# The last output tile in two column halves, and one store per block in the middle of a state-space and feed-forward kernel

## The chip, the cores and the metric

The kernel runs on one core of one Trainium2 chip. The metric is the device time of one execution in microseconds (us). The core has a matrix engine (TensorE, PE in the profile, with its weight loads listed apart as PEld), a vector engine (VectorE, DVE), a scalar engine (ScalarE, ACT), a general engine (GpSimd, POOL) and a queue processor (SyncE, SP) that here only issues DMAs. Each engine takes its instructions in the order in which the program lists them. The core's 16 DMA engines move data between the chip's main memory and the on-chip SBUF. PE writes its results to banks of PSUM, from where ACT or DVE copy them to SBUF.

## The reference

```
for each chunk of 32 tokens of each batch and head:
    L       = exp(cum_i - cum_j) for i >= j, else 0      # cum: running sum of log a
    y_intra = ((C B^T) * L) x
    y_inter = (C state) * exp(cum)
    y       = y_intra + y_inter
    state   = exp(sum of log a) * state + sum_j B_j x_j exp(cum_end - cum_j)

x   = y as (batch * tokens) x (heads * 32)               # 3072 x 256
out = (relu(x @ w_gate) * (x @ w_val)) @ w_out           # 256 -> 1536 -> 256
```

There are 4 batches, 8 heads, 768 tokens, head size 32 and state size 16. The result is 3072 x 256 in float32. The change touches only the last product, with `w_out`, and the way in which its result leaves the chip.

## The kernel before, in words

The 3072 tokens are cut into 6 blocks of 512 (`NBLK` = 6). For each block the feed-forward part computes the hidden activations `h` in 12 chunks of 128 (`gv` over 512 tokens, `gvh` over 256): PE makes gate and value in PSUM, ACT applies the relu (lines 600 and 615), and DVE multiplies (601 and 618). The first part, the state-space scan, runs over 12 pairs of 128-token chunks. Its pieces for the next block are set between the feed-forward pieces of the present one. POOL scales the loaded `B` and `C` (`scale_bc`, line 291), casts `x` (`cast_x`, line 307) and masks part of the products (`causal`, line 489).

The order of all instructions is written out by hand. The function `in_order` at the end ties each engine's instructions to the order in which the program lists them, so a reader can follow each engine from the text.

`fout(b, ts)` computes row group `ts` (128 tokens, four to a block) of block `b` of the output: 12 matmuls, one for each chunk of `h`. The chunk of `h` is the stationary operand, which is loaded anew for every matmul, and 256 columns of `w_out` stream through. Two row groups share a PSUM bank, except in the last block, where each has a bank of its own. Banks come from a rotation of five (`bank`).

`foevac(b, ts)` follows each `fout`. In blocks 1 to 4, ACT copies two row groups at once (line 652) to a buffer `ob`, and SP issues a store of 256 KB (line 653); this happens after row groups 1 and 3. In the last block each row group is copied alone (line 646), by ACT for groups 0 and 2 and by DVE for groups 1 and 3, and stored alone (line 647), 128 KB each, through ACT's DMA queue for groups 0 and 2 and through SP's for groups 1 and 3. The buffers `ob` rotate over three.

At the head of each block from 1 on, `load(n)` puts the loads of later pairs on SP's queue: six DMAs a pair (lines 116 and 117), for two pairs, up to pair 11. They are scaled by POOL some chunks later in the same block (`scale(P + 2)`) or in the next (`scale(Q)`). SP's queue is in order too, so the loads of block `b + 1` stand behind the stores of block `b`. Each DMA that SP or ACT issues adds to one of eight completion counters, which are used in rotation in the program's order. Before a DMA reuses a counter, its issuer waits for the DMA eight places earlier. At the end of the program (line 897 in the profile) SP waits for all eight counters, one after the other in their order, and then all engines meet at a barrier.

The main loop's skeleton, by which the steps can be followed:

```
for b in 1..5:
    loads of later pairs on SP
    gvh / gv chunks of block b, with transposes and scans of the next pairs between
    fout(b, 0), foevac(b, 0);  G, gevac of the next pair
    fout(b, 1), foevac(b, 1);  fout(b, 2), foevac(b, 2);  Dm, sums, yevac, G, states
    fout(b, 3), foevac(b, 3)
```

Of the kernel before, what the change touches and what calls it, by code (L numbers as in the profile page):

```python
# [8 lines left out]
FP32 = mybir.dt.float32  # L9
# [20 lines left out]
def kernel(  # L30
# [13 lines left out]
    nc = tc.nc  # L44
# [5 lines left out]
    DM, DF = moe_w_gate.shape  # L50
    T = NB * S
    NF = DF // 128
    NPAIR = T // 256
    PPB = NC // 2
    NBLK = T // 512
# [5 lines left out]
    ffn = ctx.enter_context(tc.tile_pool(name="ffn", bufs=2))  # L61
# [4 lines left out]
    def bank(name="bank", shape=(128, 512), dtype=FP32):  # L66
        return mm.tile(list(shape), dtype, tag="shared", bufs=NSHARED, name=name)
# [78 lines left out]
    for rows, base in ((slice(0, 128), 128), (slice(0, 64), 0)):  # L146
        nc.gpsimd.affine_select(
            out=wmask[rows], in_=wmask[rows], pattern=[[-1, 2], [1, 128]],
# [6 lines left out]
    for k in range(4):  # L155
# [16 lines left out]
        out=cp0, data0=a0, data1=zero1[0:R].to_broadcast([R, 128]), initial=1.0,  # L172
# [11 lines left out]
    wo = glob.tile([128, NF, DM], BF16)  # L184
# [402 lines left out]
    fst = {}  # L587
# [37 lines left out]
    def fout(b, ts):  # L625
        if ts % 2 == 0 or b == NBLK - 1:
            fst["o"] = bank("o", (128, 2, DM))
        o = fst["o"]
        for f in range(NF):
            nc.tensor.matmul(  # L630
                out=o[:, ts % 2], lhsT=fst[b][:, f, ts * 128:(ts + 1) * 128],
                rhs=wo[:, f], start=(f == 0), stop=(f == NF - 1),
                skip_group_check=True)

    def foevac(b, ts):
        last = b == NBLK - 1
        if ts % 2 == 0 and not last:
            if ts and not b:
                fst["ob"] = ob = ffn.tile([128, 2, DM], FP32, tag="ob", name="ob", bufs=3)
                nc.scalar.copy(out=ob[:, 0], in_=fst["o"][:, 0])  # L640
            return
        ob = fst.pop("ob", None) or ffn.tile([128, 2, DM], FP32, tag="ob", name="ob", bufs=3)
        r0 = b * 512 + ts * 128
        if last:
            i = ts % 2
            (nc.vector.tensor_copy if i else nc.scalar.copy)(out=ob[:, i], in_=fst["o"][:, i])
            (nc.sync if i else nc.scalar).dma_start(out=out[r0:r0 + 128, :], in_=ob[:, i])
            return
        if b == 0 and ts == 3:
            nc.scalar.copy(out=ob[:, 1], in_=fst["o"][:, 1])  # L650
        else:
            nc.scalar.copy(out=ob, in_=fst["o"])  # L652
        nc.sync.dma_start(
            out=out[r0 - 128:r0 + 128, :].rearrange("(i p) m -> p i m", p=128), in_=ob)
# [108 lines left out]
    copy_C(2, 1)  # L763
    cast_x(2, P_)
    fout(0, 0)
    foevac(0, 0)
    G_wide(2)
    adds(2)
# [9 lines left out]
    scale_bc(3, P_)  # L778
    cast_x(3, P_)
    fout(0, 1)  # L780
    foevac(0, 1)
    fout(0, 2)
    foevac(0, 2)
    inter_wide(2)
    D_wide(2)
# [116 lines left out]
```

## Time and profile before

| | |
|---|---|
| median of 6 runs | 128.15 us (127.32 to 128.64) |
| the profiled execution's own time | 127.72 us |
| its span, from first to last instruction | 126.0 us |
| PE busy | 119.6 us (95%) |
| DVE, ACT, POOL busy | 88.5, 81.7, 42.1 us |
| granted PE clock over the span | 1.000 |
| read from main memory, written to it | 11.13 MB, 3.15 MB |
| stores through SP after two row groups | 10, of 256 KB each, median 2.2 us from issue to landing |
| stores of the last block | 2 through ACT (2.1 us to landing), 2 through SP (1.7 us), 128 KB each |

A line of a group gives the source line, engine, operation and tiles, how many there were, the time in all in us and the mean of one in ns, and then the engine's idle time ahead of them with what ended it. `L630 PE` is the matmul in line 630, `L630 PEld` its weight loads. PE's records are pipelined: a matmul's record is longer than the distance to the next one, so distances are read from starts, or from the chain of waits, which is cut without overlap. A line of the timeline gives start and length in us, engine, line and operation, and in brackets the idle time before it and what released it.

### The profile page before, as it was taken

To read this page: it belongs to the slowest core of one execution; us is meant where nothing else is said; L and a number is where in the kernel's file an instruction comes from. 1 tells how busy PE (TensorE), PEld (TensorE's weight loads), DVE (VectorE), ACT (ScalarE), POOL (GpSimd) and SP (SyncE) were. 2 spreads that over 40 slices of the span, in tenths; PEclk is the share of its full clock that TensorE was granted. 3 is DMA by queue.
4 is the path that set the end of the run, shared out by engine and by line. 5 is a ranking of instruction groups with operands and counts; after the bars stand their busy time and mean duration, and the time that the engine had idled before them with its cause. 6 is when DMAs were issued, how large, how long until landed. Compare 5 with 4: busy or idle time off the path is not lost.

```text
span 126.0 us, 3627 instructions
## 1 busy us (share of the span) xinstructions
PE 119.6 (95%) x1382; PEld 83.7 (66%) x1388; DVE 88.5 (70%) x196; ACT 81.7 (65%) x184; POOL 42.1 (33%) x86
## 2 busy tenths in 40 slices
PE   6979899999999999999999999999999999999980
PEld 6856585478685478874577864577855678844870
DVE  3795888764799675989674888655988556787420
ACT  0467588835788934787935887745888647877310
POOL 6589864126535025801321704033500033000000
PEclk9999999999999999999999999999999999999999
DMA  3999999996988998597922499802200002200031
GB/s 65 208 173 203 161 219 196 156 112 79 106 96 218 111 116 90 167 122 85 105 40 88 101 107 110 104 8 83 88 0 0 0 0 88 83 0 0 5 121 46
DMA packets 72209, 12.15 MB, mean 96 GB/s; under 512 B 65936, under 2 KB 72192, under 8 KB 72192
## 3 DMA queue, kind: packets, MB, share of 16 engines
q1 hardware_dynamic: 66096, 8.91, 47.4%
q0 software_dynamic: 3184, 2.36, 12.6%
q10 hardware_dynamic: 2912, 0.66, 2.5%
q8 instruction: 11, 0.18, 0.6%
q14 instruction: 6, 0.05, 0.1%
HBM read 11.13 MB, written 3.15 MB: 113 GB/s over the span
## 4 chain that ended last, share of the span: by engine, by line
PE 85%; DMA 8%; ACT 2%; POOL 1%; issue 1%; DVE 0%; DVEq 0%; POOLq 0%
PE o L630 26%; PE gv L612 16%; PE val L597 14%; PE gate L594 12%; DMA wo<-in_moe_w_out_dram 8%; PE w L180 4%; PE y L569 2%; PE g L481 2%; PE tp L321 2%; PE y L558 1%; ACT gs L389 1%; PE g L372 1%; POOL gs L385 1%; PE A_ps L528 1%; PE y L462 1%
## 5 line engine op out<-in xcount | busy, mean ns | idle before, releaser
L601 DVE TENSOR_TENSOR h<-r,val 128x512 bf16<-128x512 bf16 x44 | 29.5, 686 | 8.8 <-ACT r L600 7.2
L630 PE MATMUL o<-wo,h 128*128 128x256 bf16 x288 | 34.2, 273 | 0.2 <-DMA wo<-in_moe_w_out_dram 0.2
L630 PEld LDWEIGHTS <-h 128*128 128x128 bf16 x288 | 27.1, 98 | 5.5 <-issue 1.5
L600 ACT ACTIVATE r<-gate 128x512 bf16<-128x512 f32 x44 | 25.9, 600 | 6.0 <-PE gate L594 4.0
L597 PE MATMUL val<-yT,wv 128*128 128x512 bf16 x88 | 26.2, 379 | 0.3
L594 PE MATMUL gate<-yT,wg 128*128 128x512 bf16 x82 | 24.9, 379 | 0.0
L618 DVE TENSOR_TENSOR h<-r,gv 128x256 bf16<-128x256 bf16 x56 | 22.5, 419 | 2.6 <-ACT r L615 1.6
L615 ACT ACTIVATE r<-gv 128x256 bf16<-128x256 f32 x56 | 21.4, 385 | 2.4 <-PE gv L612 0.4
L612 PE MATMUL gv<-yT,wv 128*128 128x256 bf16 x112 | 21.4, 273 | 0.6 <-DMA wv<-in_moe_w_val_dram 0.6
L612 PE MATMUL gv<-yT,wg 128*128 128x256 bf16 x112 | 21.4, 273 | 0.1
L489 POOL TENSOR_SCALAR_AFFINE_SELECT gs<-gs 128x512 bf16<-128x512 bf16 (+1 forms) x18 | 8.9, 520 | 32.8 <-ACT gs L500 32.8
L506 DVE TENSOR_TENSOR gs<-g,maskUT 128x512 bf16<-128x512 f32 x18 | 11.6, 686 | 11.7 <-issue 9.6
L291 POOL TENSOR_TENSOR bs<-bcr,scaleBC 128x256 bf16<-128x256 f32 x18 | 11.0, 630 | 20.5 <-PE val L597 6.0
L597 PEld LDWEIGHTS <-wv 128*128 128x128 bf16 x88 | 8.6, 98 | 10.4
L594 PEld LDWEIGHTS <-wg 128*128 128x128 bf16 x88 | 8.2, 98 | 7.0
L612 PEld LDWEIGHTS <-wv 128*128 128x128 bf16 x112 | 10.9, 98 | 2.1 <-DMA wv<-in_moe_w_val_dram 0.8
L612 PEld LDWEIGHTS <-wg 128*128 128x128 bf16 x112 | 10.2, 98 | 2.0 <-issue 0.2
L500 ACT CAST gs<-g 128x512 bf16<-128x512 f32 x9 | 5.3, 589 | 6.7 <-PE g L481 6.7
L582 ACT CAST yT<-y 128x512 bf16<-128x512 f32 x9 | 5.3, 586 | 5.3 <-PE y L569 2.7
L652 ACT COPY ob<-o 128x512 f32<-128x512 f32 x9 | 5.3, 584 | 4.1 <-PE o L630 4.1
L180 PE MATMUL w<-warm 128*128 128x128 bf16 x49 | 5.9, 296 | 1.0 <-DVE tmask L154 1.0
L180 PEld LDWEIGHTS <-warm 128*128 128x128 bf16 x58 | 5.3, 132 | 1.6 <-DVE tmask L154 1.0
(103 smaller groups left out, 118.3 us busy)
## 6 DMA issues: line engine op xcount, KB each, us to landing
out_dram<-ob SPq DMA_DIRECT2D x10, 256.0 KB, 2.2
xr<-in_x_dram SPq DMA_DIRECT2D x19, 128.0 KB, 3.7
bcr<-in_C_dram SPq DMA_DIRECT2D x19, 64.0 KB, 3.4
bcr<-in_B_dram SPq DMA_DIRECT2D x19, 64.0 KB, 3.8
wo<-in_moe_w_out_dram POOLq DMA_DIRECT2D x1, 768.0 KB, 10.7
xr<-in_x_dram SPq DMA_DIRECT2D x2, 256.0 KB, 8.0
wg<-in_moe_w_gate_dram POOLq DMA_DIRECT2D x1, 384.0 KB, 5.9
wv<-in_moe_w_val_dram POOLq DMA_DIRECT2D x1, 384.0 KB, 7.2
```

Of the source, the lines that this page charges most:

```text
L180: nc.tensor.matmul(out=w, lhsT=warm, rhs=rhs, start=True, stop=True)
L291: eng.tensor_tensor(out=bs.rearrange("s k (q t n) -> s k t q n", q=4, t=2)[:, :, t], in0=src[:, :, t], in1=f[:, :, 4 * t:4 * t + 4].to_bro ...
L489: nc.gpsimd.affine_select(out=dst, in_=dst, pattern=[[0, n], [1, 128]], compare_op=ALU.is_ge, fill=0.0, base=0, channel_multiplier=-1)
L506: nc.vector.tensor_tensor(out=d[:, q], in0=g[q], in1=m, op=ALU.mult)
L594: nc.tensor.matmul(out=g, lhsT=wg[:, k, fs], rhs=yT[:, k, tk], start=(k == 0), stop=(k == 1))
L597: nc.tensor.matmul(out=v, lhsT=wv[:, k, fs], rhs=yT[:, k, tk], start=(k == 0), stop=(k == 1))
L600: nc.scalar.activation(r, g, AF.Relu)
L601: nc.vector.tensor_tensor(out=fst[b][:, f], in0=r, in1=v, op=ALU.mult)
L612: nc.tensor.matmul(out=gv_[:, j], lhsT=w[:, k, fs], rhs=yT[:, k, tk], start=(k == 0), stop=(k == 1), skip_group_check=True)
L615: nc.scalar.activation(r, gv_[:, 0], AF.Relu)
L618: nc.vector.tensor_tensor(out=fst[b][:, f, u * 256:(u + 1) * 256], in0=r, in1=gv_[:, 1], op=ALU.mult)
L630: nc.tensor.matmul(out=o[:, ts % 2], lhsT=fst[b][:, f, ts * 128:(ts + 1) * 128], rhs=wo[:, f], start=(f == 0), stop=(f == NF - 1), skip_gr ...
```

## The change

In the last block, row group 3 (the last 128 tokens) is computed as two halves of 128 columns each: 12 matmuls for columns 0 to 127, then 12 for columns 128 to 255, with the chunk of `h` loaded for each. The second half has a PSUM bank of its own. ACT copies the first half and stores it through its own queue, and DVE copies the second half and stores it through SP's queue, 64 KB each, in rows of 512 bytes.

In blocks 1 to 3, ACT's two copies of a block go to one buffer `ob4` of four row groups (two such buffers in rotation), and SP issues one store of 512 KB after row group 3 in place of two of 256 KB after groups 1 and 3. Blocks 0 and 4 keep their two stores.

```diff
@@ fout(b, ts)
         if ts % 2 == 0 or b == NBLK - 1:
             fst["o"] = bank("o", (128, 2, DM))
         o = fst["o"]
+        if b == NBLK - 1 and ts == 3:
+            fst["oh"] = [o[:, 1, 0:128], bank("o", (128, 128))]
+            for i, oh in enumerate(fst["oh"]):
+                for f in range(NF):
+                    nc.tensor.matmul(
+                        out=oh, lhsT=fst[b][:, f, ts * 128:(ts + 1) * 128],
+                        rhs=wo[:, f, i * 128:(i + 1) * 128], start=(f == 0),
+                        stop=(f == NF - 1), skip_group_check=True)
+            return
         for f in range(NF):
@@ foevac(b, ts)
                 nc.scalar.copy(out=ob[:, 0], in_=fst["o"][:, 0])
             return
+        if 1 <= b <= 3:
+            if ts == 1:
+                fst["ob4"] = ffn.tile([128, 4, DM], FP32, tag="ob4", name="ob4")
+            ob = fst["ob4"]
+            nc.scalar.copy(out=ob[:, ts - 1:ts + 1], in_=fst["o"])
+            if ts == 3:
+                nc.sync.dma_start(
+                    out=out[b * 512:(b + 1) * 512, :].rearrange("(i p) m -> p i m", p=128),
+                    in_=ob)
+            return
         ob = fst.pop("ob", None) or ffn.tile([128, 2, DM], FP32, tag="ob", name="ob", bufs=3)
         r0 = b * 512 + ts * 128
+        if last and ts == 3:
+            for i, (eng, q) in enumerate(((nc.scalar.copy, nc.scalar),
+                                          (nc.vector.tensor_copy, nc.sync))):
+                cs = slice(i * 128, (i + 1) * 128)
+                eng(out=ob[:, 1, cs], in_=fst["oh"][i])
+                q.dma_start(out=out[r0:r0 + 128, cs], in_=ob[:, 1, cs])
+            return
         if last:
```

## The prediction

> **What bounds the kernel now.** I read the page's engine table first, then the chain of waits to its end, then the end itself in stretches.
>
> ```profile
> PE 119.6 (95%) x1382; PEld 83.7 (66%) x1388; DVE 88.5 (70%) x196; ACT 81.7 (65%) x184; POOL 42.1 (33%) x86
> ```
>
> TensorE (PE) is busy 119.6 us of 126.0, at full granted clock in every slice. From 100 us on, the chain of waits is one unbroken row of PE pieces; it ends like this (start, length, what):
>
> ```profile
> 116.33 0.43 PE gate L594 x2
> 116.76 0.43 PE val L597 x2
> 117.19 5.25 PE o L630 x48
> 122.45 0.03 DVEq L646
> 122.48 0.04 issue
> 122.53 0.42 DVE ob L646
> ```
>
> So two things can shorten this kernel: less PE time, or a shorter end behind the last matmul. The end is 126.0 - 122.5 = 3.5 us in which no engine computes except for one copy, as the busy time by stretch shows (after the stretch: length, then PE, PEld, DVE, ACT, POOL, clock, DMA share, GB/s):
>
> ```profile
> 122.00:123.00 1.00, 0.44 (x4) 0.14 (x2) 0.42 (x1) 0.00 (x0) 0.00 (x0) 1.00 0.39 131
> 123.00:124.00 1.00, 0.00 (x0) 0.00 (x0) 0.00 (x0) 0.00 (x0) 0.00 (x0) 1.00 0.15 51
> 124.00:125.00 1.00, 0.00 (x0) 0.00 (x0) 0.00 (x0) 0.00 (x0) 0.00 (x0) 1.00 0.24 80
> 125.00:126.00 1.00, 0.00 (x0) 0.00 (x0) 0.00 (x0) 0.00 (x0) 0.00 (x0) 1.00 0.00 0
> ```
>
> The trace's instruction and packet records split it: copy 122.53 to 122.95; SP starts the store at 122.98; its packets run from 123.83 to 124.34; SP's wait for it passes at 124.70; then SP checks the remaining completion counters of the DMAs one by one, about 0.06 us each, until 125.07; drains and the last barrier take until 125.96.
>
> **The change, part by part.**
>
> *The last tile's matmuls.* Twelve pairs of weight load and 256-column matmul become 24 pairs of weight load and 128-column matmul: the same columns, twice the loads. A 256-column pair costs 5.25/48 = 0.109 us. What a 128-column pair costs is the main question, because every such pair loads a full 128x128 tile of weights, and the loads' records last 98 ns. These rows hold the nearest case, transposes (128 columns, a new 128x128 weight tile each): first the groups, then one piece of the chain.
>
> ```profile
> L630 PE MATMUL o<-wo,h 128*128 128x256 bf16 x288 | 34.2, 273 | 0.2 <-DMA wo<-in_moe_w_out_dram 0.2
> L321 PE MATMUL tp<-ident,bs 128*128 128x128 bf16 x44 | 4.6, 223 | 0.0
> L321 PEld LDWEIGHTS <-bs 128*128 128x128 bf16 x48 | 3.5, 99 | 2.7
> ```
> ```profile
> 75.45 0.22 PE tp L321 x4
> ```
>
> Four pairs in 0.22 us: 55 ns each, although the load's record is 99 ns, so loads overlap each other's records and the matmuls. Seven warm-up pairs at 7.0 us start 55.6 to 56 ns apart in the records. With 55.6: 24 x 0.0556 = 1.334 against 12 x 0.109 = 1.31; +0.03 us. Here a rule speaks against the change. The Trainium skill, "TensorE: Matmul & The Clock Gate", section "Back-to-back issue gap", says that a sustained stream of load and matmul pairs runs at about 81 ns per 128-column matmul, and that the 56 ns gap leaves the loads out. By it the tile takes 24 x 0.081 = 1.94 us, +0.63. The row has loads in it and decides: I take 55.6 ns; 81 ns is an end of the range, since the row's bursts are 4 to 7 pairs and this one is 24.
>
> *The evacuations.* The first half is ready 12 pairs, 12 x 0.0556 = 0.67 us, before the second. ScalarE (ACT) is free after issuing the store of row group 2 (121.56 + 0.36 = 121.93); its half copy, between 164 ns for 6 columns (L224) and 373 ns for 256 (L646), is by straight line 0.27 us, done at 122.24, and its store starts near 122.27. It also waits for row group 0's store, whose buffer it reuses: issued at 118.94, last packet 120.98; passed by 121.4. Behind it on ACT stands only its own store. That half lies beside the second one, which sets the end. There VectorE (DVE) copies 128 columns in place of 256:
>
> ```profile
> L646 DVE COPY ob<-o 128x256 f32<-128x256 f32 x2 | 0.8, 425 | 4.0 <-PE o L630 4.0
> L667 DVE COPY wfac<-fac 128x48 f32<-128x48 f32 x1 | 0.2, 208 | 0.6 <-PE fac L209 0.6
> ```
>
> (425 - 208)/208 = 1.04 ns per column, so 425 - 128 x 1.04 = 0.291 us: -0.134. Bounds: -0.21 (half) to 0. In the program as built it waits on no ACT copy of this tile; if it did, ACT is done at 122.24, before the 122.55 at which DVE starts anyway.
>
> *The last store.* Still 128 rows, so I leave its issue (0.345 us) and the time to the first packet (0.85 us) as they are; each row has 512 B in place of 1024. In the packet records a 1024 B packet takes 46 ns and a 512 B one on the same queue (the 48 of the load of `a`) 25 to 27 ns. Eight packets on each of 16 DMA engines: 8 x 46 = 0.37 to 8 x 26 = 0.21 us, -0.16. Bounds: -0.2 to 0 (packets of half the size at the old duration).
>
> *The final checks.* Hardware DMAs count on eight counters in rotation, and SP's last checks go through these in order. Before, the last store counts on counter 1, checked at 124.70; six more checks follow it. The change removes three DMAs (blocks 1 to 3) and adds one: two fewer, so the last store moves from counter 1 to (1 - 2) mod 8 = 7, which is checked last. The other checks then lie under the wait. -(125.07 - 124.70) = -0.37 us. The first half's store is on counter 6, some 0.6 us ahead of the last. Bounds: -0.37 to 0, should the end be held by something else.
>
> *One store per block in blocks 1 to 3.* Each takes an SP issue and a 256 KB transfer away after row group 1 and makes the one after row group 3 512 KB. The copies on ACT stay, same sizes (0.58 us each). On SP nothing stood between the two stores, so nothing is passed; behind the larger one stand the next block's twelve loads (blocks 1 and 2). 256 KB more is 16 packets of 1 KB per engine, 16 x 46 = 0.74 us, so loads land up to 0.74 us later, by shared engines or by a counter's wait. Who notices? GpSimd (POOL), which scales them:
>
> ```profile
> 59.29 1.20 POOL L291 TENSOR_TENSOR bs<-bcr,scaleBC 128x256 bf16<-128x256 f32 x2 [5.96 <-PE val L597]
> 65.32 0.99 POOL L489 TENSOR_SCALAR_AFFINE_SELECT gs<-gs 128x512 bf16<-128x512 bf16 x2 [4.28 <-ACT gs L500]
> 77.22 1.20 POOL L291 TENSOR_TENSOR bs<-bcr,scaleBC 128x256 bf16<-128x256 f32 x2 [5.68 <-PE gate L594]
> 83.68 0.99 POOL L489 TENSOR_SCALAR_AFFINE_SELECT gs<-gs 128x512 bf16<-128x512 bf16 x2 [4.71 <-ACT gs L500]
> ```
>
> Both scalings wait for PE, not for data: the four loads they need have landed by 57.5 and 76.0, 1.8 and 1.2 us ahead. Past that, POOL idles 4.3 and 4.7 us before the mask that is queued next. Cost 0; without this cover, the 0.74 us twice. Gain also 0: no engine waits for these stores or for SP.
>
> *Sum,* on the profiled execution (127.72, span 125.96): +0.03 - 0.13 - 0.16 - 0.37 = -0.63 us, span about 125.3. What lies around the span stays. The median of the runs shown is 128.15, 0.43 above the profiled one; the difference carries over: 127.5 us.
>
> **Rivals.** A change of 0.5% (0.64 us) is about what a measurement of this kernel can tell from none.
>
> 1. *Part of the end doesn't come.* The final checks were not what held the end, or the half-sized packets bring nothing: 127.7 to 127.9. For it: both terms come from records of one execution. Against it: the six checks stand in a row with nothing else in flight.
> 2. *The weight loads show.* 81 ns per pair takes back 0.61 us: 128.1. For it: the rule above, no row with 24 such pairs. Against it: 55 ns in every burst.
> 3. *Slower: the weight loads bind.* If a pair cannot go below the 0.109 us that it takes now, the tile takes 2.62 us, +1.31, less 0.66 for the rest: 128.8. It decides from the pitch at which the tile's growth eats 0.66 us: (1.31 + 0.66)/24 = 82 ns. For it: 98 ns loads twice as often. Against it: the 55 ns row, whose loads are as long.
> 4. *The split or the merged stores do nothing:* a DVE half that waits for ACT, or loads that turn late. The first costs nothing by the times above; the second must exceed 1.2 + 4.7 us before a mask moves. About 128.15 if all else failed too.
>
> **How the numbers follow.** Likeliest (0.66): all terms near their values, 127.5, own range 127.1 to 127.8; its centre is on the 0.5% line (127.51), and I count 0.50 of it as faster, since no term is rounded up, and 0.16 as same. Rivals 1 and 4 0.15 and rival 2 0.09, nearly all same; rival 3 0.10, slower at 128.8. Faster 0.51, same 0.39, slower 0.10. The range for 8 in 10 runs from 126.9 (all bounds of the gains and a measurement's own spread) to 128.4 (past rival 2, short of rival 3).
>
> **What would show it.** Right: 24 matmuls of 128 columns 55 to 56 ns apart; DVE's last copy near 0.29 us from 122.55; the last store's landing at 1.5 us in place of 1.7; less than 1.0 us from SP's last DMA wait to the end in place of 1.26; POOL's scalings still released by PE. Wrong: a pitch of 80 ns or more, a last copy of 0.4 us, a wait of PE for POOL or a load in blocks 2 to 4, or an end after the landing as long as now.

## The result, and the profile after

The changed kernel takes 127.5 us (median of 35 runs, 126.87 to 128.47) against 128.28 us for the kernel before (72 runs). The ratio is 0.9944, with a 95% interval from 0.9931 to 0.9956: 0.72 us less, between 0.56 and 0.88. That is 0.56% less, by its middle value a little more than the 0.5% that the prediction took for the least that a measurement of this kernel can tell from none; the small end of the interval, 0.44%, lies below that. The time is the forecast one.

PE's share has not moved. From the page of the changed kernel:

```profile
PE 119.1 (95%) x1394; PEld 83.4 (66%) x1400; DVE 88.2 (70%) x196; ACT 82.2 (65%) x185; POOL 42.4 (34%) x86
```

The end of its chain of waits (start, length, what):

```profile
117.24 0.43 PE val L597 x2
117.67 3.93 PE o L639 x36
121.60 1.35 PE o L633 x24
122.96 0.04 DVEq L667
122.99 0.04 issue
123.03 0.29 DVE ob L667
```

The 24 pairs of 128 columns (line 633) take 1.35 us and the copy 0.29. Behind the last matmul only this copy is left, and the span ends at 125.8 in place of 126.0:

```profile
123.00:124.00 1.00, 0.00 (x0) 0.00 (x0) 0.29 (x1) 0.00 (x0) 0.00 (x0) 1.00 0.55 176
124.00:125.00 1.00, 0.00 (x0) 0.00 (x0) 0.00 (x0) 0.00 (x0) 0.00 (x0) 1.00 0.23 66
125.00:126.00 1.00, 0.00 (x0) 0.00 (x0) 0.00 (x0) 0.00 (x0) 0.00 (x0) 1.00 0.00 0
```

The two profiled executions didn't start alike. The first matmul of the output (row group 0 of block 0) starts at 25.34 us after and 24.86 before, in a part of the program that the change doesn't touch. In the ten executions whose traces are used here that start lies between 24.7 and 26.3. So spans are not compared here. What is compared is a distance inside the trace: from the first matmul of the last row group to the end. It is 4.999 us before and 4.370 after, 0.629 us less. Between block 0 and the last row group nothing changed: from the first output matmul of one block to that of the next it is 19.352, 18.561, 18.360, 18.324, 17.573 us before and 19.353, 18.561, 18.360, 18.321, 17.574 after.

The instruction and packet records split the 4.999 and the 4.370 us like this:

| step | before, us | after, us | difference | predicted |
|---|---|---|---|---|
| first matmul of the row group to the start of DVE's copy | 1.566 | 1.597 | +0.03 | +0.03 |
| DVE's last copy | 0.425 | 0.291 | -0.134 | -0.134 |
| end of the copy to the start of SP's store | 0.028 | 0.027 | 0 | 0 |
| start of the store to its last packet | 1.355 | 1.190 | -0.165 | -0.16 |
| last packet to SP's wait for it passing | 0.368 | 0.375 | +0.01 | 0 |
| from there to the end | 1.257 | 0.890 | -0.367 | -0.37 |

The largest step is the last one. The instruction records give the times at which SP's eight checks at the end of the program passed (us; the check of the last store's counter in bold):

| counter | 0 | 1 | 2 | 3 | 4 | 5 | 6 | 7 | end of the span |
|---|---|---|---|---|---|---|---|---|---|
| before | 123.43 | **124.70** | 124.77 | 124.83 | 124.89 | 124.95 | 125.01 | 125.07 | 125.96 |
| after | 123.80 | 123.87 | 123.93 | 124.00 | 124.05 | 124.12 | 124.41 | **124.92** | 125.81 |

Before, six more checks of about 0.06 us each stand behind the wait for the last store. After, all the others stand ahead of it; counter 6 is that of the first half's store.

### The profile page after: what moved, and what is told of

It reads as the page before. It is cut to its first block, busy times and chain, and to the rows that moved or that the text cites. A ratio compares the mean times of both kernels' runs of the same rounds, so it can differ in the third digit from the quotient of the medians.

```text
span 125.8 us, 3642 instructions
## 1 busy us (share of the span) xinstructions
PE 119.1 (95%) x1394; PEld 83.4 (66%) x1400; DVE 88.2 (70%) x196; ACT 82.2 (65%) x185; POOL 42.4 (34%) x86
## 4 chain that ended last, share of the span: by engine, by line
PE 80%; DMA 9%; POOL 7%; issue 1%; DVE 1%; DVEq 0%; POOLq 0%
PE o L639 25%; PE gv L612 16%; PE val L597 14%; PE gate L594 12%; DMA wo<-in_moe_w_out_dram 9%; PE y L569 2%; PE g L481 2%; PE w L180 2%; POOL wg L189 2%; POOL wv L189 2%; POOL bs L277 2%; PE tp L321 2%; PE y L558 1%; PE o L633 1%; POOL gs L385 1%
## 5 line engine op out<-in xcount | busy, mean ns | idle before, releaser
L639 PE MATMUL o<-wo,h 128*128 128x256 bf16 x276 | 32.8, 273 | 0.6 <-DMA wo<-in_moe_w_out_dram 0.6
L639 PEld LDWEIGHTS <-h 128*128 128x128 bf16 x276 | 25.9, 98 | 5.7 <-issue 1.5
L597 PE MATMUL val<-yT,wv 128*128 128x512 bf16 x88 | 26.2, 379 | 0.6 <-DMA wv<-in_moe_w_val_dram 0.3
L597 PEld LDWEIGHTS <-wv 128*128 128x128 bf16 x88 | 8.5, 98 | 10.7 <-DMA wv<-in_moe_w_val_dram 0.6
L180 PE MATMUL w<-warm 128*128 128x128 bf16 x49 | 5.3, 277 | 1.0 <-DVE tmask L154 1.0
L540 DVE TENSOR_TENSOR Sm<-A_ps,smask 128x256 bf16<-128x256 f32 x15 | 5.7, 416 | 0.0
## 6 DMA issues: line engine op xcount, KB each, us to landing
xr<-in_x_dram SPq DMA_DIRECT2D x19, 128.0 KB, 3.8
```

Of the source, the lines that this page charges most:

```text
L180: nc.tensor.matmul(out=w, lhsT=warm, rhs=rhs, start=True, stop=True)
L597: nc.tensor.matmul(out=v, lhsT=wv[:, k, fs], rhs=yT[:, k, tk], start=(k == 0), stop=(k == 1))
L639: nc.tensor.matmul(out=o[:, ts % 2], lhsT=fst[b][:, f, ts * 128:(ts + 1) * 128], rhs=wo[:, f], start=(f == 0), stop=(f == NF - 1), skip_gr ...
```

## The experiments

Each was run beside the kernel before on the same chip. Times are medians and ratios are to the kernel before; a tail is the distance from the first matmul of the last row group to the end, in the one execution that was traced.

**The halves alone.** The block with `if 1 <= b <= 3:` is taken out of the changed kernel:

```diff
-        if 1 <= b <= 3:
-            if ts == 1:
-                fst["ob4"] = ffn.tile([128, 4, DM], FP32, tag="ob4", name="ob4")
...
```

> The two column halves alone; blocks 1 to 3 keep their two stores each. One DMA more than before, so the last store counts on counter 2 in place of 1 and five checks follow it. Theory (copy -0.13, packets -0.16, matmuls +0.08 less 0.05 of the shorter last record, checks -0.06): about 0.32 us less than the kernel before, 128.0, and from the last row group's first matmul to the end 4.68 us (before 5.00, changed kernel 4.37). If the halves are the whole gain: 127.5 and 4.37 us. If the merged stores are the gain: no more than 0.26 us less.

Measured: 128.0 us, ratio 0.9979 (0.996 to 0.9998), tail 4.700 us. The pair distance, the copy (0.292) and the store (1.188 to the last packet) are those of the changed kernel. After SP's wait for the last store the program runs on for 1.194 us, 0.304 longer than in the changed kernel: five checks. So the halves give 0.3 us and not the whole gain.

**The merged stores alone.** The changes to the last tile are taken out:

```diff
-        if b == NBLK - 1 and ts == 3:
-            fst["oh"] = [o[:, 1, 0:128], bank("o", (128, 128))]
...
-        if last and ts == 3:
-            for i, (eng, q) in enumerate(((nc.scalar.copy, nc.scalar),
...
```

> The merged stores of blocks 1 to 3 alone; the last tile as before. Three DMAs fewer, so the last store counts on counter 6 and one check follows it. Theory: the store itself lands as before, the checks give 0.31 us: 128.0, and 4.69 us from the last row group's first matmul to the end, the middle of the kernel unchanged. If the halves are the whole gain: as before, 128.3 and 5.00 us. If less store traffic in the middle were the gain: PE's work between 40 and 105 us gets shorter, and the end stays at 5.00 us.

Measured: 127.92 us, ratio 0.9977 (0.9959 to 0.9994), tail 4.696 us. The distances between blocks are 19.354, 18.561, 18.360, 18.324, 17.573 us: nothing in the middle is shorter. The store takes 1.352 us to its last packet, as before; what is gone is 0.305 us between the wait for it and the end.

**More stores in place of fewer.** Into the kernel before, ahead of the store of two row groups:

```diff
+        if 1 <= b <= 3:
+            for i in range(2):
+                nc.sync.dma_start(out=out[r0 - 128 + i * 128:r0 + i * 128, :], in_=ob[:, i])
+            return
         nc.sync.dma_start(
```

> The opposite of merging, and no halves: each of the six stores of blocks 1 to 3 is cut in two of 128 KB. Six DMAs more than before, so the last store counts on counter (1 + 6) mod 8 = 7, checked last. Theory: 0.37 us less than the kernel before, about 127.9, and 4.63 us from the last row group's first matmul to the end, though there are more stores. If fewer stores are what helps: as before or slower, 5.00 us.

Measured: 128.15 us, tail 4.632 us, as expected. The ratio is 0.9977 with an interval that just reaches no change (0.9949 to 1.0005). The tail is the firmer witness: six DMAs more take 0.367 us off the end, because they move the last store to the counter that is checked last. This and the run before it settle which part of the merging counts.

**One store more in the changed kernel.**

```diff
+        if b == 4 and ts == 1:
+            for i in range(2):
+                nc.sync.dma_start(out=out[r0 - 128 + i * 128:r0 + i * 128, :], in_=ob[:, i])
+            return
         nc.sync.dma_start(
```

> The changed kernel with one thing different: block 4's first store of 256 KB is cut in two, so the last store counts on counter 0, and seven checks follow it. Theory: 7 x 0.061 = 0.43 us of the gain goes: about 127.95, and 4.80 us from the last row group's first matmul to the end (changed kernel 4.37). If the place of the last check doesn't matter: 127.5 and 4.37 us.

Measured: 128.14 us, ratio 0.9977 (0.9953 to 1.0001), tail 4.792 us. From SP's wait for the last store to the end it is 1.330 us, 0.44 us more than in the changed kernel, and the tail is 0.42 us longer: most of the gain is gone with one DMA more, which has nothing to do with the tile.

**All row groups of the last block in halves.** In `fout`, ahead of the loop of 256-column matmuls:

```diff
+        if b == NBLK - 1:
+            for i in range(2):
+                cs = slice(i * 128, (i + 1) * 128)
+                for f in range(NF):
+                    nc.tensor.matmul(
+                        out=o[:, ts % 2, cs], lhsT=fst[b][:, f, ts * 128:(ts + 1) * 128],
+                        rhs=wo[:, f, cs], start=(f == 0 and i == 0), stop=(f == NF - 1),
+                        skip_group_check=True)
+            return
         for f in range(NF):
```

> The changed kernel with all four row groups of the last block computed in two column halves (96 pairs of weight load and 128-column matmul in a row; copies and stores as in the changed kernel). It asks what a long row of such pairs costs. Theory (the changed kernel's 24 pairs stand 55.8 ns apart): 96 x 0.0558 = 5.36 us in place of 5.28, about 127.6. By the 81 ns of the rule that spoke against the change: 7.78 us, about 130.0.

Measured: 128.69 us, ratio 1.0038 (0.9983 to 1.0094). Neither expectation was met. The tail is 4.376 us and the pairs stand 55 to 56 ns apart, so the time went elsewhere. The end of this kernel's chain of waits:

```profile
116.77 0.45 PE gate L594 x2
117.22 0.02 issue
117.24 0.61 ACT r L600
117.85 0.02 issue
117.87 0.70 DVE h L601
118.57 0.05 issue
118.62 3.58 PE o L642 x61
122.20 1.35 PE o L633 x24
```

and its weight loads in the timeline, with the idle time before the second group:

```profile
117.26 0.82 PEld L642 LDWEIGHTS <-h 128*128 128x128 bf16 x11
118.61 3.41 PEld L642 LDWEIGHTS <-h 128*128 128x128 bf16 x61 [0.54 <-DVE h L601]
```

The chain leaves PE: the first 11 pairs are through in 0.6 us, and the twelfth waits for the last chunk of `h`, which ACT and DVE finish at 118.57. With 256-column pairs the same eleven take 1.2 us, and this last chunk has just been made: in the changed kernel it is ready at 118.60, 0.11 us ahead of the twelfth matmul. The slower pairs had hidden 0.5 us of ACT's and DVE's work. In the trace, the four row groups and the end take 8.937 us from the first output matmul of the block, against 8.300 in the changed kernel.

**Halves in row groups 1 to 3 only.** The same edit, with `b == NBLK - 1 and ts`:

```diff
-        if b == NBLK - 1:
+        if b == NBLK - 1 and ts:
```

> The kernel with all row groups of the last block in halves had PE wait 0.54 us for DVE's last piece of h, because the first 12 pairs of row group 0 went by in 0.61 us in place of 1.2. Here row group 0 keeps its 12 pairs of 256 columns, and groups 1 to 3 are computed in halves (72 pairs in a row). If that wait was the cause: no wait, 72 x 0.0558 + 12 x 0.109 = 5.33 us for the four row groups against 5.28 in the changed kernel, 127.55. If long rows of 128-column pairs cost more by themselves: 0.5 us or more above that, 128 or more.

Measured: 127.39 us, ratio 0.9948 (0.9923 to 0.9974); 8.356 us from the first output matmul of the block, 0.056 more than in the changed kernel. Its chain never leaves PE:

```profile
116.64 0.43 PE val L597 x2
117.07 1.31 PE o L648 x12
118.38 2.68 PE o L642 x48
121.06 1.35 PE o L633 x24
```

72 pairs in a row at 4.03/72 = 56 ns. The wait for `h` was the cause of the miss, and a long row of such pairs costs no more than a short one.

**A cut at column 192.**

```diff
-            fst["oh"] = [o[:, 1, 0:128], bank("o", (128, 128))]
+            fst["oh"] = [o[:, 1, 0:192], bank("o", (128, 64))]
+            cut = (0, 192, 256)
...
-                        rhs=wo[:, f, i * 128:(i + 1) * 128], start=(f == 0),
+                        rhs=wo[:, f, cut[i]:cut[i + 1]], start=(f == 0),
...
-                cs = slice(i * 128, (i + 1) * 128)
+                cs = slice((0, 192)[i], (192, 256)[i])
```

> The changed kernel with the last tile cut at column 192: 12 pairs of 192 columns for ACT's part, then 12 pairs of 64 for DVE's. DVE's copy 0.29 to 0.225 us, packets of 256 bytes 0.21 to 0.14 us. If a 64-column pair costs its columns (29 ns): the matmuls as now, and 0.14 us less, about 127.35. If a pair cannot go below the 55 ns of a 128-column one: 12 x 0.026 = 0.31 us more for the matmuls, 0.17 us more in all, about 127.7.

Measured: 127.36 us, ratio 0.9941 (0.9894 to 0.9988), tail 4.277 us, 0.093 less than in the changed kernel. A 192-column pair takes 82 to 83 ns and a 64-column pair 29, each with its own load of 128x128 weights, whose records still last 98 ns:

```profile
L634 PEld LDWEIGHTS <-h 128*128 128x128 bf16 x24 | 1.5, 98 | 0.0
L634 PE MATMUL o<-wo,h 128*128 128x192 bf16 x12 | 1.2, 246 | 0.0
L634 PE MATMUL o<-wo,h 128*128 128x64 bf16 x12 | 0.5, 193 | 0.0
```

Of the 0.14 us that were expected, the copy (0.224) and the store (1.124 to the last packet) came; 0.04 us were lost between the last packet and SP's wait passing (0.411 in place of 0.375). The cut need not be the cause: with the halves alone, whose last tile is that of the changed kernel, this step took 0.404. This version has the shortest tail of all, but by less than the times can tell from the changed kernel. ACT's store of 192 columns passes only 0.165 us before the last one, so a cut further right would probably soon make it the end; none was run.

**The loads held back more.**

```diff
-        if 1 <= b <= 3:
+        if 1 <= b <= 4:
...
-            if ts == 3:
+            for _ in range(0 if ts != 3 else 2 if b == 1 else 1):
                 nc.sync.dma_start(
```

> The changed kernel with block 1's 512 KB store issued twice (the same data to the same place) and block 4's two stores merged, so that the number of DMAs and the counter of the last store stay. The loads behind block 1's store are held back by another 32 x 46 ns = 1.47 us. Theory: POOL scales the next pair about 1.5 us later, which eats into its idle time of 3.3 us before the mask that follows; PE notices nothing, 127.5. If the delay of loads reaches PE: up to 1.5 us more, 129.

Measured: 127.63 us, ratio 0.9956 (0.9911 to 1.0002), tail 4.372 us, distances between blocks as in the changed kernel (19.349, 18.561, 18.360, 18.320, 17.572). POOL shows the delay. First the changed kernel, then the one with the store issued twice:

```profile
60.36 1.20 POOL L291 TENSOR_TENSOR bs<-bcr,scaleBC 128x256 bf16<-128x256 f32 x2 [6.56 <-DMA bcr<-in_C_dram]
65.80 0.99 POOL L489 TENSOR_SCALAR_AFFINE_SELECT gs<-gs 128x512 bf16<-128x512 bf16 x2 [3.31 <-ACT gs L500]
```
```profile
63.59 1.20 POOL L291 TENSOR_TENSOR bs<-bcr,scaleBC 128x256 bf16<-128x256 f32 x2 [9.31 <-DMA bcr<-in_C_dram]
66.26 0.99 POOL L489 TENSOR_SCALAR_AFFINE_SELECT gs<-gs 128x512 bf16<-128x512 bf16 x2 [0.92 <-ACT gs L500]
```

POOL starts the scaling later and its idle time before the mask falls from 3.31 to 0.92 us, by more than the 1.5 expected. The edit did more than add a transfer: SP issued the second store only at 55.76, 2.94 us after the first, when the first had landed (55.74) and its counter, for which the second waits, was full. The last load for the scaling landed 2.85 us later than in the changed kernel, counted from the first matmul of the output. The mask is still released by ACT, and PE notices nothing, so the test was harder than planned and the answer the same.

## Why the prediction was right, point by point

- *The last tile's matmuls.* Right: 55.8 ns per pair, +0.03 us to the start of the copy. The rule of 81 ns for a sustained row, which the prediction cites, did not hold here, neither in the 24 pairs nor in the 72 in a row. The 98 ns record of a weight load was no bound: pairs of 64 columns go at 29 ns. Rivals 2 and 3 fall.
- *The evacuations.* DVE's half copy took 0.291 us, as worked out from the two rows. ACT's half copy took 0.266 (0.27). Wrong was "passed by 121.4" for row group 0's store: in this execution its last packet came at 121.97 and it had landed at 122.47. The group's line puts ACT's 0.53 us of idle time ahead of the half copy down to it, but for 0.36 us of these ACT was issuing the store of row group 2, which isn't counted as busy (122.04 to 122.40 in the timeline); the landing came 0.06 us after that. So the wait for it was short, and it cost nothing, because SP's check of that half's counter passed 0.51 us before the last one.

```profile
L667 DVE COPY ob<-o 128x128 f32<-128x128 f32 x1 | 0.3, 291 | 2.3 <-PE o L633 2.3
L667 ACT COPY ob<-o 128x128 f32<-128x128 f32 x1 | 0.3, 266 | 0.5 <-DMA out_dram<-ob 0.5
```
```profile
122.04 0.36 ACTq L673 DMA_DIRECT2D out_dram<-ob  x1
122.54 0.27 ACT L667 COPY ob<-o 128x128 f32<-128x128 f32 x1 [0.53 <-DMA out_dram<-ob]
```

- *The last store.* Right: the issue still takes 0.345 us, the first packet comes after 0.840, a 512-byte packet takes 27 ns where one of 1024 took 46 to 47, and 0.165 us are saved.
- *The final checks.* Right, and shown by the four runs that change the number of DMAs, and with it the last store's counter: 1.257 us from the wait to the end on counter 1, 1.194 on counter 2, 0.952 on counter 6, 0.890 on counter 7, and 1.330 on counter 0. It is the largest term of the sum, and an accident of the count: the change removed two DMAs from the rotation. Rival 1 falls with it.
- *One store per block.* Cost and gain 0 came true, but of the two covers the first was misread. The loads for the scalings had not landed by 57.5 and 76.0. In the kernel before, the last of the four landed at 59.13 and 76.92, 0.16 and 0.31 us ahead of the scalings at 59.29 and 77.22, and in all ten executions the scaling starts 0.16 to 0.31 us after that landing. So both scalings waited for data before the change too. The `PE val L597` in brackets belongs to another counter that POOL tests ahead of the same scaling, and "POOL's scalings still released by PE" could not serve as a sign. The cost was 0 by the second cover alone, POOL's idle time ahead of the mask. In the changed kernel the last load lands 0.51 us later in block 2 and 0.74 in block 3, counted from the first matmul of the output, which is within the 0.74 worked out; the idle time falls from 4.28 to 3.31 us and from 4.71 to 4.07, and the mask of block 2 starts 40.5 us after that first matmul in all ten executions. Not all of the 0.51 need be the merging: where it was run once, this load landed 34.27 to 34.77 us after the first matmul of the output, with separate stores 34.17 to 34.36. Rival 4 needed more than 4.3 us in block 2, not 6; it falls with the store issued twice.
- *The sum.* -0.63 predicted, -0.629 in the trace's tail. The ratio of the times says -0.72 (-0.88 to -0.56), which holds 0.63; what the rest of 0.09 us is, if it is anything, these runs can't tell. That 127.5 was met to the tenth is in part luck: the kernel before came out at 128.28 in place of the 128.15 that was used, and the medians lie 0.78 us apart in place of 0.63.

## What to carry to other kernels

When PE runs without a gap, read the end behind its last matmul instruction by instruction, down to the order in which the program checks its outstanding DMAs: a store that is checked early in that order is followed by every later check. Cutting the last tile pays: 0.26 of the 0.63 us here, the other 0.37 being the count of DMAs. Cutting the row groups before it brought nothing, and where row group 0 was cut as well, PE became faster while ACT and DVE were still making its input, and the gain turned into a wait. Where a time depends on the number of DMAs modulo the number of counters, compare two versions only after looking at which counter the last one has.

## What was not expected of the hardware

A load of 128x128 weights in front of each matmul cost nothing that could be seen down to 64 columns: a pair takes 109, 82.5, 56 and 29 ns with 256, 192, 128 and 64 columns, 26.7 ns for every 64, which leaves 2 to 3 ns for all that doesn't depend on the columns. One check of a completion counter costs about 61 ns, (1.257 - 0.890)/6.

And a fetch of instructions seems to hold a store up. In the changed kernel's packet records, a fetch of 16 KB in one packet lasts from 120.33 for 0.92 us. Of row group 0's store, fifteen of the sixteen parts are through by 120.80; the eight packets of the last one start only at 121.24, when the fetch is ending, and it is through at 121.97. In nine of the ten executions this store's last part ends 0.7 us after such a fetch; in the tenth (all row groups in halves) the fetch was over ahead of the store's first packet, and the sixteen parts end within 0.33 us of one another. The records used here don't name the DMA engine of a packet, so that the fetch and the late part share one is inferred from these times. The page counts these fetches:

```profile
q8 instruction: 11, 0.18, 0.5%
```
